# A transformer block's MLP: the second norm of token blocks 2 and 3 turned by VectorE and DMAs

## The chip, the cores and the metric

The kernel runs on one core of one Trainium2 chip. The core has TensorE (PE; its weight loads are a row of their own, PEld), VectorE (DVE), ScalarE (ACT), GpSimd (POOL) and SyncE (SP, which here issues the DMAs), with an on-chip memory of 128 partitions (SBUF), accumulation banks (PSUM) and device memory. The metric is the device time of one execution in microseconds (us), the median of several runs; lower is better.

## The reference

One block on x of 2048 tokens by 576 features, conditioned by six rows (`sa`, `ca`, `ga`, `sb`, `cb`, `gb`) worked out from a small vector `c`:

```
h = layernorm(x) * (1 + ca) + sa
x = x + ga * attention(h, wq, wk, wv, wo)          # 32 heads of 18, one shared k and v
h = layernorm(x) * (1 + cb) + sb                   # the "second norm"
y = layernorm(h)
x = x + gb * (gelu(y @ w1 + b1) @ w2 + b2)         # 576 -> 4608 -> 576
```

Everything is fp32. The second norm is in fact two norms, one behind the other (`h`, then `y`), with two rows between them.

## The kernel before, in words

**Layout.** The 2048 tokens are four blocks of 512 (`TB`), each of four tiles of 128 tokens. The residual `XT` holds tokens on the partitions. The first product of the MLP needs `y` the other way round, with features on the partitions: `yr` (128 x 10 x 512 for a pair of blocks, `KD` = 5 slices of 128 features per block, the fifth half used and filled with a second copy of its 64 features). So each tile of 128 tokens x 576 features must be normed twice and turned.

**The MLP in visits.** The MLP works on pairs of blocks: blocks 0 and 1, then blocks 2 and 3. For each pair it makes 18 visits (`NG`), each of 256 of the 4608 hidden features, 36 in all; I number them v0 to v35. A 2 x 2 scheme with seven products in place of eight is used for both matrices, and each fp32 product is made of a high and a low part. In a visit PE makes seven products of the first matrix (A11, S2, S3, A12, S1, A22, S4; `product`, L1156, into the PSUM banks `psB`) and, between them, the seven groups of the visit before for the second matrix (`fc2s`, L1247 to L1265): a group is twice 12 matmuls into one of two `psA` slots, and each slot is emptied by one DVE add (L1265). ACT and DVE make the gelu, POOL the sums and low parts (L1225 to L1233). The ACT copy at L1392 stands once near the start of each visit, so it marks its length.

**Weights.** `load_w1` (L788 to L792) and `load_w2s` (L1218 to L1223) are issued by SP, each right behind the product that used the buffer, for the next visit: there is one buffer of each, and a load has about a visit to land. SP runs its DMAs in written order.

**The end of a pair.** Visits v16, v17 and v35 make the second matrix whole (`fc2`, L1293). In v17 `op_pieces` (L1051, copies at L1069, subtractions at L1071) makes the operand pieces of blocks 2 and 3 out of `yr`: `+B11` is the first copy, `-B11` the DVE subtraction behind it.

**The second norm of blocks 2 and 3.** It is made during v1 to v16, in the gaps of the engines. `more` (L1366) is called seven times in each visit (behind A11, S2, S3, A12, S1, A22 and S4), and steps the generator `ln2_pair` (L701) once. The stages of a tile (`ln2_stages`, L658) are: `stats` (DVE: two BN_STATS and a BN_AGGR), `scale` (three small POOL operations), `norm` (ACT), `rows` (two POOL operations of 128 x 576), `stats` and `scale` again, `renorm` (two ACT operations, and b2 added to the residual on POOL), and `turn`: PE transposes (`transpose_tile`, L155 of its helper) into a `psB` bank, four of 128 columns in one step and the fifth in the next, each step emptied by ACT into `yr`. Eight tiles make 40 transposes. Tile i begins 10 steps behind tile i-1; steps with a turn are held to the third and fourth calls of a visit (`room`, `mark`). At the end two POOL operations of 128 x 1024 (L714, L716) make two sums of `yr` slices that the seven-product scheme needs.

Of the kernel before, what the change touches and what calls it, by code (L numbers as in the profile page):

```python
# [8 lines left out]
F32 = mybir.dt.float32  # L9
F32R = mybir.dt.float32r  # L10
AF = mybir.ActivationFunctionType
ALU = mybir.AluOpType
AX = mybir.AxisListType

S, D, H, DH, F = 2048, 576, 32, 18, 4608
NB = 4
TB = S // NB
NT = TB // 128
KD = 5
# [4 lines left out]
NG = F // 256  # L24
# [8 lines left out]
def block_kernel(ctx: ExitStack, tc, x, wqkv, wo, w1, b1, w2, b2, c, wmod, ident_in, out):  # L33
    nc = tc.nc
    ve, ac, po, pe, sy = nc.vector, nc.scalar, nc.gpsimd, nc.tensor, nc.sync
# [39 lines left out]
    BC = per.tile([128, 3, D], F32, name="BC")  # L75
# [5 lines left out]
    at = tc.tile_pool(name="at", bufs=1, side="right")  # L81
# [74 lines left out]

    def transpose_tile(Z, yr, t, k0, k1, e):
        p = psB()
        for k in range(k0, k1):
            tr(p[:, 128 * (k - k0):128 * (k - k0 + 1)], Z, k)  # L160
        n = k1 - k0
        src = p[:, :128 * n].rearrange("p (k c) -> p k c", k=n)
        dst = yr[:, k0:k1, 128 * t:128 * (t + 1)]
        if e is ac:
            ac.activation(dst, src, AF.Copy)
        else:
            ve.tensor_copy(dst, src)
# [329 lines left out]
    px = pxp.__enter__()  # L497
# [160 lines left out]
    def ln2_stages(tb, t):  # L658

        X = XT[:, NT * tb + t, :]  # L660
        o = {}

        def small(n):
            return per.tile([128, n], F32, name="sm2", bufs=8)

        def stats(i):
            src = o["h"] if i else X
            o["mv", i] = small(2)
            stt = ln_stats1(src)
            ve.bn_stats(stt[:, 1, :], src[:, 288:])  # L670
            ve.bn_aggr(o["mv", i], stt)

        def scale(i):
            mv, rs, nb = o["mv", i], small(1), small(1)
            po.tensor_scalar(rs, mv[:, 1:2], EPS, None, op0=ALU.add)
            po.tensor_tensor(rs, rs, nhalf, op=ALU.pow)
            po.tensor_scalar(nb, mv[:, 0:1], rs, -1.0, op0=ALU.mult, op1=ALU.mult)
            o["sc", i] = dict(scale=rs, bias=nb)

        def norm():  # L680
            Z = o["Z"] = px.tile([128, 640], F32, name="Z2", bufs=2)
            o["h"] = Z[:, :D]
            ac.activation(o["h"], X, AF.Identity, **o["sc", 0])

        def rows():
            po.tensor_mul(o["h"], o["h"], BC[:, 1, :])
            po.tensor_tensor(o["h"], o["h"], BC[:, 0, :], op=ALU.add)

        def renorm():
            ac.activation(o["Z"][:, D:], o["Z"][:, 512:D], AF.Identity, **o["sc", 1])  # L690
            ac.activation(o["h"], o["h"], AF.Identity, **o["sc", 1])
            po.tensor_tensor(X, X, B2["b"], op=ALU.add)

        def turn(k0, k1, e):
            yr = YR[tb // 2][:, KD * (tb % 2):KD * (tb % 2 + 1)]
            transpose_tile(o["Z"], yr, t, k0, k1, e)

        return {0: lambda: stats(0), 1: lambda: scale(0), 4: norm, 5: rows, 8: lambda: stats(1), 9: lambda: scale(1),
                12: renorm, 14: lambda: turn(0, 4, ac), 15: lambda: turn(4, 5, ac)}

    def ln2_pair():  # L701
        YR[1] = per.tile([128, 2 * KD, TB], F32, name="yr", tag="big", bufs=3)
        at = {}
        for _ in range(2):
            yield
        for i in range(2 * NT):
            for k, f in ln2_stages(2 + i // NT, i % NT).items():
                at.setdefault(10 * i + k, []).append((k >= 14, f))
        for k in range(max(at) + 1):
            for _, f in at.get(k, ()):  # L710
                f()
            yield "T" if any(t for t, _ in at.get(k + 1, ())) else None
        R = YR[1]
        po.tensor_tensor(R[:, 5:7], R[:, 7:9], R[:, 5:7], op=ALU.subtract)  # L714
        yield
        po.tensor_tensor(R[:, 5:7], R[:, 5:7], R[:, 0:2], op=ALU.add)  # L716
        yield

    def wo_mm(tb, t, h2, p, k0, k1, end=KD, first=0):
        A = ATT[tb]  # L720
# [190 lines left out]
    def step(q):  # L911
        if q:
            try:
                return next(q[0])
            except StopIteration:
                q.popleft()
# [218 lines left out]
    def load_w2(v):  # L1135
        w = W2[WHOLE[v]]
        if len(w) < 4:
            w.extend(px.tile([128, 640], F32R, name="Z2", bufs=2)[:, :D] for _ in range(2))
        for l in range(2):
            for f in range(2):  # L1140
                sy.dma_start(w[2 * l + f].bitcast(F32), w2scr[v % NG, :, l, f])
# [193 lines left out]
                        load_w2s(0, k)  # L1335
            yield

    fill = deque([ln2_pair()])
    f2 = deque()
    gens, sm = deque(), deque()  # L1340
    between2 = [None]
# [12 lines left out]
                gens.remove(gen)  # L1354

    form = op_pieces(YR[0], po)
    mark = [None]

    for v in range(NV):
        nxt = (v + 1) % NG  # L1360
        if v == NG - 1:
            while fill:
                step(fill)
            form = op_pieces(YR[1], po)

        def more(half="", first="", room=False):  # L1366

            if v in (0, NG - 1, NG):
                form(first if v == 0 else half if v == NG - 1 else {"+T4": "-T4 +T1 -B22", "-T4": "-T1 -t1"}.get(first, ""))
            elif v > NG + 1 and fill:  # L1370
                step(fill)
            elif 0 < v < NG and fill and (room or mark[0] != "T" or v == NG - 2):
                mark[0] = next(fill[0], "end")
                if mark[0] == "end":
                    fill.popleft()
            if v == 0 and rest:
                for _ in range(2):
                    if rest:
                        wo_tile(*rest.popleft())
                if not rest:  # L1380
                    wo_end()

        def w_(w):
            if v + 1 < NV:
                load_w1(nxt, w)

        if v == NG + 1:
            fill.append(pair_end())
        ba = psB()
        product(ba, "A11", 0)  # L1390
        w_("A11")
        ac.activation(U[:, 0], ba, AF.Copy)  # L1392
        g_()
        s_()
        more("+B11", "+T4")
        bb = psB()
        product(bb, "S2", 6, mid=t_ if v > 1 and v - 1 not in WHOLE and v - 2 not in WHOLE else None)
        w_("S2")
        ve.tensor_tensor(U[:, 0], bb, U[:, 0], op=ALU.add)
        if v != 1:  # L1400
            t_()
        g_()
        more("-B11 +T2", "-T4")
        bc = psB()
        product(bc, "S3", 10)
        w_("S3")
        ve.tensor_tensor(U[:, 1], bc, U[:, 0], op=ALU.add)
        s_()
        more("-T2 =T3", "+B22", True)
        if v != 1:  # L1410
            t_()
        product(ba, "A12", 2, False, (0, 0))
        w_("A12")
        gens.append(gelu(v, 0, 0, ba))
        g_()
        s_()
        more("+T3 +B21", "-B22", True)
        t_()
        g_()
        bd = psB()  # L1420
        product(bd, "S1", 8, True, (1, 1))
        w_("S1")
        be = psB()
        ve.tensor_tensor(be, bd, U[:, 1], op=ALU.add)
        g_()
        gens.append(gelu(v, 1, 1, be))
        g_()
        more("-T3 -B21")
        t_()
        g_()  # L1430
        product(bc, "A22", 12, False, (1, 0), t_ if v == 1 else None)
        w_("A22")
        ve.tensor_tensor(bc, bc, U[:, 0], op=ALU.add)
        g_()
        gens.append(gelu(v, 1, 0, bc))
        g_()
        more("=T4 +t0")
        t_()
        if v - 1 in WHOLE:
            t_()  # L1440
        g_()
        product(bd, "S4", 4, False, (2, 1), t_ if v == 1 else None)
        w_("S4 tails")
        if v == NV - 1:
            t_(lambda: (eb_add(NV - 2, 1, 1, (0,)), g_()))
        ve.tensor_tensor(bd, bd, U[:, 0], op=ALU.add)
        if v < NV - 1:
            g_()
        gens.append(gelu(v, 0, 1, bd))
        g_()  # L1450
        if v < NV - 1:
            t_()
        more("=T1 +T4 -t0 +B22 +t1")
        if v == NV - 1:
            last = fc2(v)
            next(last)
            t_(lambda: next(last))
            for to in ((1, 0, (1,)), (1, 1, (1,))):
                eb_add(NV - 2, *to)
            while gens:  # L1460
                g_()
            eb_add(NV - 2, 0, 1)
            f2.append(last)
            continue
        if v - 1 in WHOLE:
            while f2:
                t_()
        if v not in WHOLE:
            sm.append(sums(v))
            s_()  # L1470
            f2.append(fc2s(v))
        else:
            f2.append(fc2(v))
# [42 lines left out]
```

## Time and profile before

| | |
|---|---|
| median of 3 runs | 2223.07 us (2222.27 to 2224.61) |
| profiled execution, its own time | 2222.87 us |
| its span | 2221.0 us |
| busy: PE, PEld, DVE, ACT, POOL | 99%, 65%, 87%, 74%, 69% |
| MLP visits of the first pair | v0 to v17, some 23 us each |
| 40 PE transposes, L155 | inside v3 to v16 |

The span is what the hardware profiler saw from the first instruction to the last; 1.9 us lie around it. Busy shares are means over stages that differ, so a visit has to be read by itself.

### The profile page before, as it was taken

How to read it: one execution, taken by the hardware profiler on the slowest of the kernel's cores; microseconds unless marked ns; L12 is line 12 of the kernel's file. 1: busy time of each engine (PE TensorE's matmuls, PEld its weight loads, DVE VectorE, ACT ScalarE, POOL GpSimd, SP SyncE). 2: the span in 40 equal slices, each digit the busy share in tenths (PEclk: the TensorE clock that was granted, in tenths of full speed). 3: DMA queues.
4: the chain of work that ended last, by engine and by line, in shares of the span. 5: the costliest groups of instructions: out<-in, count | busy, mean ns of one | idle time of the engine just before them, and what ended most of it. 6: DMA issues, size and time to landing. Idle time of an engine off the chain costs nothing.

```text
span 2221.0 us, 46122 instructions
## 1 busy us (share of the span) xinstructions
PE 2201.4 (99%) x16643; PEld 1449.3 (65%) x16643; DVE 1932.7 (87%) x3415; ACT 1639.2 (74%) x3144; POOL 1526.4 (69%) x1762
## 2 busy tenths in 40 slices
PE   8999999999999999999999999999999999999999
PEld 5654444444544545444454446888888899889898
DVE  7689999999999999999999983888888878788887
ACT  5569999999999999999999998544445444343443
POOL 7654455666776687678676540888888867877776
PEclk9999999999999999999999999999999999999999
DMA  6242143443333332333333321666666646676663
GB/s 228 86 133 92 34 134 117 135 129 116 126 119 118 115 130 97 112 130 111 117 127 117 120 70 63 207 178 175 179 179 180 184 128 182 180 219 189 178 183 123
DMA packets 184632, 307.71 MB, mean 139 GB/s; under 512 B 19695, under 2 KB 75391, under 8 KB 184405
## 3 DMA queue, kind: packets, MB, share of 16 engines
q1 hardware_dynamic: 184261, 304.62, 43.9%
q8 instruction: 132, 2.16, 0.4%
q14 instruction: 95, 0.78, 0.1%
q10 hardware_dynamic: 144, 0.15, 0.0%
HBM read 200.68 MB, written 93.79 MB: 133 GB/s over the span
## 4 chain that ended last, share of the span: by engine, by line
PE 93%; DVE 1%; ACT 1%; issue 0%; ACTq 0%; DVEq 0%
PE psC L932 24%; PE psB L1156 18%; PE psA L1259 16%; PE psB L942 14%; PE psM L319 13%; PE psB L731 2%; PE psB L952 2%; PE psA L1293 1%; PE psA L731 1%; PE psB L155 0%; PE psB L248 0%; PE psB L357 0%; PE psM L942 0%; ACT P L944 0%; DVE mx L344 0%; DVE gs L1168 0%
## 5 line engine op out<-in xcount | busy, mean ns | idle before, releaser
L944 ACT ACTIVATE P<-psB 128x512 f32<-128x512 f32 x2013 | 1054.4, 619 | 42.3 <-PE psM L319 20.6
L964 DVE TENSOR_REDUCE mx<-psM 128x1 f32<-128x512 f32 x1476 | 934.3, 682 | 28.5 <-PE psM L319 15.6
L942 PE MATMUL psB<-qst,KS 64*128 64x512 f32 x2013 | 605.1, 433 | 0.1
L319 PE MATMUL psM<-KS,qst 64*128 64x512 f32 x1722 | 590.2, 434 | 0.7 <-DVE mx L337 0.2
L932 PE MATMUL psC<-P,V 128*32 128x256 f32 (+3 forms) x6608 | 568.1, 439 | 0.0
L942 PEld LDWEIGHTS psB<-qst,KS 64*128 64x128 f32 x2013 | 301.7, 184 | 218.6 <-ACT P L944 186.2
L319 PEld LDWEIGHTS psM<-KS,qst 64*128 64x128 f32 x1722 | 283.5, 184 | 185.6 <-DVE mx L964 130.3
L1156 PE MATMUL psB<-ops,w1a 128*128 128x512 f32 x1512 | 393.9, 396 | 0.2 <-DVE h L1171 0.2
L1156 PEld LDWEIGHTS psB<-ops,w1a 128*128 128x128 f32 x1512 | 270.1, 188 | 46.7 <-DVE h L1171 0.6
L932 PEld LDWEIGHTS psC<-P,V 128*32 128x32 f32 x6608 | 147.0, 108 | 187.7 <-issue 160.2
L1265 DVE TENSOR_TENSOR XT<-psA,XT 128x576 f32<-128x576 f32 x330 | 241.8, 753 | 18.6 <-PE psA L1259 13.2
L1259 PEld LDWEIGHTS psA<-w2s,big 128*128 128x128 f32 x1584 | 223.0, 188 | 14.0 <-POOL big L1233 2.5
L1259 PE MATMUL psA<-w2s,big 128*128 128x288 f32 x1584 | 230.5, 294 | 0.0
L1169 ACT ACTIVATE psB<-gs 128x512 f32<-128x512 f32 x144 | 86.7, 602 | 127.6 <-DVE gs L1168 127.4
L1233 POOL TENSOR_TENSOR big<-s,big 128x512 fp32r<-128x512 f32 x132 | 171.0, 1295 | 10.6
L962 DVE CUSTOM_DVE_ANT_0 xc<-psM,xc 128x512 f32<-128x512 f32 x246 | 166.3, 682 | 12.9 <-PE psM L319 4.4
L1165 ACT ACTIVATE h<-psB,b1t 128x512 f32<-128x512 f32 x144 | 98.1, 681 | 100.7 <-PE psB L1156 76.7
L768 POOL TENSOR_TENSOR os<-O,os 128x512 fp32r<-128x512 f32 x31 | 39.8, 1285 | 171.8 <-ACT os L767 171.8
L955 ACT ACTIVATE xc<-psB 128x512 f32<-128x512 f32 x246 | 154.1, 626 | 3.0 <-PE psM L319 0.2
L1168 DVE SCALAR_TENSOR_TENSOR gs<-psB,h 128x512 f32<-128x512 f32 x144 | 98.6, 684 | 38.5 <-ACT psB L1166 38.4
L802 POOL TENSOR_TENSOR r<-r,r 128x256 fp32r<-128x256 f32 (+1 forms) x162 | 121.8, 752 | 13.0
L1174 ACT ACTIVATE big<-h 128x512 fp32r<-128x512 f32 x39 | 24.7, 634 | 133.8 <-DVE h L1171 133.8
(217 smaller groups left out, 3327.5 us busy)
## 6 DMA issues: line engine op xcount, KB each, us to landing
w1a<-w1scr SPq DMA_DIRECT2D x252, 256.0 KB
w2s<-w2sum SPq DMA_DIRECT2D x132, 288.0 KB
w1scr<-r SPq DMA_DIRECT2D x126, 256.0 KB
w2s<-w2scr SPq DMA_DIRECT2D x76, 288.0 KB
w2scr<-r SPq DMA_DIRECT2D x72, 288.0 KB
w2sum<-r SPq DMA_DIRECT2D x72, 288.0 KB
qst<-qscr SPq DMA_DIRECT2D x192, 72.0 KB
w1a<-w2scr SPq DMA_DIRECT2D x33, 288.0 KB
```

What stands on the lines that cost most here:

```text
L319: pe.matmul(o, QST[n][64 * g:64 * g + 64, p, 128 * qt:128 * (qt + 1)], KS[64 * g:64 * g + 64, 512 * kb:512 * (kb + 1)], start=True, stop=True)
L802: po.tensor_tensor(o[:, n:2 * n], src, o[:, :n].bitcast(F32), op=ALU.subtract)
L932: pe.matmul(PVt[n][32 * j:32 * (j + 1), cs], V[:, kc, :], t[:, j, cs], start=(kc == 0 and h0 == 0), stop=(kc == 15), skip_group_check=True)
L942: pe.matmul(t, KS[64 * g:64 * g + 64, 128 * kc:128 * (kc + 1)], QST[n][64 * g:64 * g + 64, i, :], start=True, stop=True)
L944: ac.activation(P[n, kc][:, 2 * i + g, :], t, AF.Exp, scale=SCALE)
L955: ac.activation(XC[-1], t, AF.Relu)
L962: ve.tensor_tensor_reduce(c, t, c, 1.0, -3.0e38, ALU.add, ALU.max, o)
L964: ve.tensor_reduce(o, t, axis=AX.X, op=ALU.max)
L1156: pe.matmul(o, x, y, start=(first and i == 0), stop=(i == len(terms) - 1), skip_group_check=True)
L1233: po.tensor_tensor(unit(u, 1), x, unit(u, 0).bitcast(F32), op=ALU.subtract)
L1259: pe.matmul(p[:, i, :288], x[:, ts_], W2S[k][:, y], start=(bool(first) and q == 0), stop=(q == 2), skip_group_check=True)
L1265: ve.tensor_tensor(o, p[:, :, :288], o, op=ALU.add)
```

## The change

The eight tiles of blocks 2 and 3 are no longer turned by PE.

- `turn` is one DVE operation for a tile, `ve.transpose` of 128 x 576 (L693 of the new file), which turns each 32 x 32 square in its place. Its result goes to `T`, a third row of the tile `BC`. There is one `T`.
- `spread` (L695) brings the squares to their partitions of `yr`: 24 DMAs from SBUF to SBUF per tile, all issued by SP, six at each of four calls. Per tile there are 8 of 32 x 5 x 32 elements (L702), 8 of 32 x 4 x 32 (L704) and 8 of 32 x 32 (L707). A contiguous piece is 32 fp32 values, 128 bytes, so a tile has 8 x 160 + 8 x 128 + 8 x 32 = 2,560 pieces; the eight tiles make 192 DMAs.
- The copy of the last 64 features (one ACT operation of 128 x 64 per tile) and the ACT emptying of the PE transposes go; the tile buffer `Z2` is 576 wide in place of 640.
- `less` makes the two sums on POOL per 128 tokens (128 x 2 x 128 elements) instead of 128 x 1024 at the end, each for tokens t of both blocks.
- The generator with its marks is replaced by `ln2_plan`: a table `when` gives each tile the visits of its five steps. `turn` stands at the third call of visits 4, 5, 8, 9, 12, 13, 15 and 16, and the spreads at calls four to seven of the same visit; `stats`, `scale`, `rows`, `norm` and `renorm` get calls of their own. The last `less` stands at the start of v17, ahead of the first copy of `op_pieces`.

The core of the diff:

```diff
@@ ln2_stages
         def norm():
-            Z = o["Z"] = px.tile([128, 640], F32, name="Z2", bufs=2)
-            o["h"] = Z[:, :D]
+            o["h"] = px.tile([128, D], F32, name="Z2", bufs=2)
             ac.activation(o["h"], X, AF.Identity, **o["sc", 0])
...
         def renorm():
-            ac.activation(o["Z"][:, D:], o["Z"][:, 512:D], AF.Identity, **o["sc", 1])
             ac.activation(o["h"], o["h"], AF.Identity, **o["sc", 1])
             po.tensor_tensor(X, X, B2["b"], op=ALU.add)
 
-        def turn(k0, k1, e):
-            yr = YR[tb // 2][:, KD * (tb % 2):KD * (tb % 2 + 1)]
-            transpose_tile(o["Z"], yr, t, k0, k1, e)
...
+        def turn():
+            ve.transpose(T, o["h"])
+
+        def spread(i):
+            yr = YR[1][:, KD * (tb % 2):KD * (tb % 2 + 1), 128 * t:128 * (t + 1)]
+            for n in range(i, 24, 4):
+                p, q = divmod(n, 6)
+                rs, cs = slice(32 * p, 32 * p + 32), slice(32 * p, 32 * p + 32)
+                if q < 2:
+                    sy.dma_start(yr[32 * q:32 * q + 32, :, cs], wide[rs, :, 64 + 32 * q:96 + 32 * q])
+                elif q < 4:
+                    sy.dma_start(yr[32 * q:32 * q + 32, :KD - 1, cs],
+                                 T[rs, :512].rearrange("f (k c) -> f k c", c=128)[:, :, 32 * q:32 * q + 32])
+                else:
+                    sy.dma_start(yr[32 * q - 64:32 * q - 32, KD - 1, cs], T[rs, 32 * q + 384:32 * q + 416])
+
+        def less():
+            R = YR[1][:, :, 128 * t:128 * (t + 1)]
+            po.tensor_tensor(R[:, 5:7], R[:, 7:9], R[:, 5:7], op=ALU.subtract)
+            po.tensor_tensor(R[:, 5:7], R[:, 5:7], R[:, 0:2], op=ALU.add)
+
+        T = BC[:, 2, :]
...
+    def ln2_plan():
...
+        when = ((1, 1, 2, 3, 4), (2, 2, 3, 4, 5), (5, 5, 6, 7, 8), (6, 6, 7, 8, 9), (9, 9, 10, 11, 12, 13, 6),
+                (10, 10, 11, 12, 13, 15, 4), (11, 12, 13, 14, 15, 16, 5), (13, 13, 14, 15, 16, NG - 1, 0))
+        turns = [w[4] for w in when]
+        for i, (v0, v1, v2, v3, v4, *end) in enumerate(when):
+            stats, scale, norm, rows, renorm, turn, spread, less = ln2_stages(2 + i // NT, i % NT)
+            at(v0, 4, stats, 0)
+            at(v1, 5, scale, 0)
+            at(v1, 6, norm)
+            at(v2, 4, rows)
+            at(v3, 4 if v3 in turns else 3, stats, 1)
+            at(v3, 5, scale, 1)
+            at(v3, 6, renorm)
+            at(v4, 3, turn)
+            for j in range(4):
+                at(v4, 4 + j, spread, j)
+            if end:
+                at(*end, less)
+        return plan
...
     for v in range(NV):
         nxt = (v + 1) % NG
+        calls = iter(range(1, 8))
+        if v == 1:
+            plan = ln2_plan()
         if v == NG - 1:
-            while fill:
-                step(fill)
+            planned(v, 0)
             form = op_pieces(YR[1], po)
...
-            elif 0 < v < NG and fill and (room or mark[0] != "T" or v == NG - 2):
-                mark[0] = next(fill[0], "end")
-                if mark[0] == "end":
-                    fill.popleft()
+            elif 0 < v < NG:
+                planned(v, next(calls))
```

The lines of the MLP stand 26 lower in the new file (L1265 becomes L1291, L792 becomes L818, L1223 becomes L1249).

What stands on SP in the middle of a visit of the first pair, before: the loads of the next visit's weights alternate, L792 those of the first matrix (the second `w1a` row here is that of A12) and L1223 those of the second.

```order
L1223 DMA w2s<-w2sum 128x576
L792 DMA w1a<-w1scr 128x512
L1223 DMA w2s<-w2scr 128x2x288
L792 DMA w1a<-w1scr 128x512
L1223 DMA w2s<-w2scr 128x2x288
L792 DMA w1a<-w1scr 128x512
```

The same place in a visit with a turn, now: `BC` is the row `T`, `yr` the operand of blocks 2 and 3.

```order
L1249 DMA w2s<-w2sum 128x576
L818 DMA w1a<-w1scr 128x512
L702 DMA yr<-BC 32x5x32
L707 DMA yr<-BC 32x32
L704 DMA yr<-BC 32x4x32
L702 DMA yr<-BC 32x5x32
L707 DMA yr<-BC 32x32
L704 DMA yr<-BC 32x4x32
L1249 DMA w2s<-w2scr 128x2x288
L818 DMA w1a<-w1scr 128x512
```

Six DMAs have come between the A12 load and the loads behind it; three more batches of six follow in the visit, each behind the next `w1a` load.

What stands on DVE at the start of visits in which a tile gets its second `stats`, before: `psA` adds (L1265) around the three stats operations, and the second gelu operation (L1168) and the S2 addition (L1399) of the visit.

```order
L1171 SCALAR_TENSOR_TENSOR h<-psB,h 128x512
L1265 TENSOR_TENSOR XT<-psA,XT 128x2x288 x2
L143 BN_STATS bst<-Z 128x6
L670 BN_STATS bst<-Z 128x6
L671 BN_AGGR sm<-bst 128x2
L1168 SCALAR_TENSOR_TENSOR gs<-psB,h 128x512
L1265 TENSOR_TENSOR XT<-psA,XT 128x2x288 x2
L1399 TENSOR_TENSOR u<-psB,u 128x512
```

On DVE in v5, the second of two visits with a turn, now (L1437 is the addition behind S3, L1407 before; L1197 and L1194 are the gelu's).

```order
L1197 SCALAR_TENSOR_TENSOR h<-psB,h 128x512
L1437 TENSOR_TENSOR u<-psB,u 128x512
L693 STREAM_TRANSPOSE BC<-Z 128x576
L1291 TENSOR_TENSOR XT<-psA,XT 128x2x288 x2
L143 BN_STATS bst<-XT 128x6
L670 BN_STATS bst<-XT 128x6
L671 BN_AGGR sm<-bst 128x2
L1291 TENSOR_TENSOR eb<-psA,eb 128x576 x2
L1194 SCALAR_TENSOR_TENSOR gs<-psB,h 128x512
```

The stats have left the start of the visit for its middle, and the turn stands ahead of two adds that empty `psA` slots.

## Rows read from the trace of the kernel before

**Rows 1.** The page, busy time of each engine: us, share of the span, instructions.

```profile
PE 2201.4 (99%) x16643; PEld 1449.3 (65%) x16643; DVE 1932.7 (87%) x3415; ACT 1639.2 (74%) x3144; POOL 1526.4 (69%) x1762
```

**Rows 2.** Two visits by window: length, busy PE PEld DVE ACT POOL, clock, DMA share, GB/s.

```profile
1450.00:1500.00 50.00, 50.00 (x297) 44.69 (x297) 39.63 (x62) 23.49 (x40) 44.19 (x45) 1.00 0.62 177
```

**Rows 3.** ACT timeline, L1392, v3, v16, v21, v22: start, duration, engine, line, [idle before].

```profile
1442.92 0.60 ACT L1392 ACTIVATE u<-psB 128x512 f32<-128x512 f32 x1
...
1744.16 0.60 ACT L1392 ACTIVATE u<-psB 128x512 f32<-128x512 f32 x1
...
1862.13 0.60 ACT L1392 ACTIVATE u<-psB 128x512 f32<-128x512 f32 x1 [0.18 <-PE psB L1156]
...
1884.91 0.60 ACT L1392 ACTIVATE u<-psB 128x512 f32<-128x512 f32 x1 [0.17 <-PE psB L1156]
```

**Rows 4.** PEld timeline, the two turns of one tile in a visit.

```profile
1494.80 0.59 PEld L155 LDWEIGHTS psB<-ident,Z 128*128 128x128 f32 x4
...
1498.71 0.14 PEld L155 LDWEIGHTS psB<-ident,Z 128*128 128x128 f32 x1
```

**Rows 5.** Waits of PEld, 1400 to 2200 us: us in total, times, longest.

```profile
PEld psA L1259 <- POOL big L1233: 2.5, 7, 0.4
```

**Rows 6.** SP timeline of the visit that begins at 1466.27.

```profile
1466.27 0.32 SPq L792 DMA_DIRECT2D w1a<-w1scr  x1
...
1475.43 0.32 SPq L792 DMA_DIRECT2D w1a<-w1scr  x1
1477.52 0.52 SPq L1223 DMA_DIRECT2D w2s<-w2scr  x1
...
1487.86 0.32 SPq L1223 DMA_DIRECT2D w2s<-w2sum  x1
```

**Rows 7.** Lines of SP: count, ns min/median/max, starts; last row timeline of one four.

```profile
L772 SPq DMA_DIRECT2D big<-os x112: 765/789/897, 203.4 to 1351.9; - x112
L779 SPq DMA_DIRECT2D big<-os x12: 697/711/775, 469.0 to 1084.9; - x12
L364 SPq DMA_DIRECT2D qst<-ms x128: 620/638/911, 125.7 to 1332.2; - x128
L315 SPq DMA_DIRECT2D qst<-qscr x192: 265/313/1562, 39.2 to 1264.7; - x192
...
316.02 3.33 SPq L772 DMA_DIRECT2D big<-os  x4
```

**Rows 8.** Waits of SP for a DMA to land: us in total, times, longest.

```profile
SPq L540 <- DMA rowscr<-bc: 3.0, 3, 1.0
```

**Rows 9.** DVE's transposes of the attention and its stats, by line.

```profile
L749 DVE STREAM_TRANSPOSE T<-O x32: 700/702/711, 174.6 to 1372.9; 128x512 f32<-128x512 f32 x32
...
L143 DVE BATCH_NORM_STATS2 bst<-Z x16: 449/450/460, 555.6 to 1744.7; 128x6 f32<-128x288 f32 x16
```

**Rows 10.** DVE and PEld timelines of v21, which begins at 1862.13.

```profile
1868.09 0.69 DVE L1407 TENSOR_TENSOR u<-psB,u 128x512 f32<-128x512 f32 x1
...
1871.11 1.78 PEld L1259 LDWEIGHTS psA<-w2s,gt 128*128 128x128 f32 x12
...
1872.36 1.56 DVE L1265 TENSOR_TENSOR BC<-psA,BC 128x576 f32<-128x576 f32 x2 [1.93 <-PE psA L1259]
```

**Rows 11.** ACT, DVE and PEld timelines of v17.

```profile
1768.24 0.61 ACT L1392 ACTIVATE u<-psB 128x512 f32<-128x512 f32 x1
...
1769.46 1.05 ACT L1069 ACTIVATE ops<-yr 128x1024 fp32r<-128x1024 f32 x1
...
1771.96 2.38 DVE L1071 TENSOR_TENSOR ops<-yr,ops 128x1024 fp32r<-128x1024 f32 x1
...
1777.64 1.41 DVE L1330 TENSOR_TENSOR XT<-psA,XT 128x576 f32<-128x576 f32 x2
...
1778.57 0.55 PEld L1293 LDWEIGHTS psA<-w2s,gt 128*128 128x128 f32 x3
```

**Rows 12.** The page, the queue of SP's DMAs: packets, MB, share of 16 engines.

```profile
q1 hardware_dynamic: 184261, 304.62, 43.9%
```

More of the change, by code (lines that the diff above doesn't have):

```diff
@@ L689, in renorm @@
         def renorm():
-            ac.activation(o["Z"][:, D:], o["Z"][:, 512:D], AF.Identity, **o["sc", 1])
             ac.activation(o["h"], o["h"], AF.Identity, **o["sc", 1])
             po.tensor_tensor(X, X, B2["b"], op=ALU.add)
-        def turn(k0, k1, e):
-            yr = YR[tb // 2][:, KD * (tb % 2):KD * (tb % 2 + 1)]
-            transpose_tile(o["Z"], yr, t, k0, k1, e)
-        return {0: lambda: stats(0), 1: lambda: scale(0), 4: norm, 5: rows, 8: lambda: stats(1), 9: lambda: scale(1),
-                12: renorm, 14: lambda: turn(0, 4, ac), 15: lambda: turn(4, 5, ac)}
@@ L701, in ln2_pair @@
-    def ln2_pair():
-        YR[1] = per.tile([128, 2 * KD, TB], F32, name="yr", tag="big", bufs=3)
[L703 to L717, printed above, removed]
+        def turn():
+            ve.transpose(T, o["h"])
@@ new lines, in less, with at @@
+        def less():
[3 more added lines that the diff above has]
+        T = BC[:, 2, :]
+        wide = BC.rearrange("p r d -> p (r d)")[:, 2 * D - 64:].rearrange("f (k c) -> f k c", c=128)
+        return stats, scale, norm, rows, renorm, turn, spread, less
+    def ln2_plan():
+        YR[1] = per.tile([128, 2 * KD, TB], F32, name="yr", tag="big", bufs=3)
+        plan = {}
+        def at(v, c, f, *a):
+            plan.setdefault((v, c), []).append(lambda: f(*a))
+        when = ((1, 1, 2, 3, 4), (2, 2, 3, 4, 5), (5, 5, 6, 7, 8), (6, 6, 7, 8, 9), (9, 9, 10, 11, 12, 13, 6),
[16 more added lines that the diff above has]
+        return plan
@@ L1137, in load_w2 @@
         if len(w) < 4:
-            w.extend(px.tile([128, 640], F32R, name="Z2", bufs=2)[:, :D] for _ in range(2))
+            w.extend(px.tile([128, D], F32R, name="Z2", bufs=2) for _ in range(2))
         for l in range(2):
@@ L1336, in fc2 @@
             yield
-    fill = deque([ln2_pair()])
+    fill = deque()
+    plan = {}
     f2 = deque()
@@ L1356, in block_kernel, with planned, more @@
     form = op_pieces(YR[0], po)
-    mark = [None]
+    def planned(*when):
+        for f in plan.pop(when, ()):
+            f()
     for v in range(NV):
         nxt = (v + 1) % NG
+        calls = iter(range(1, 8))
+        if v == 1:
+            plan = ln2_plan()
         if v == NG - 1:
-            while fill:
-                step(fill)
+            planned(v, 0)
             form = op_pieces(YR[1], po)
-        def more(half="", first="", room=False):
+        def more(half="", first=""):
             if v in (0, NG - 1, NG):
@@ L1408, in block_kernel @@
         s_()
-        more("-T2 =T3", "+B22", True)
+        more("-T2 =T3", "+B22")
         if v != 1:
@@ L1416, in block_kernel @@
         s_()
-        more("+T3 +B21", "-B22", True)
+        more("+T3 +B21", "-B22")
         t_()
```

## The prediction

> **What bounds the kernel now.** The page first: PE is busy 99% of the span and every other engine less [rows 1], so a gain must come out of PE's own work or its few waits, and a loss is whatever makes PE wait. Second the stage: the change touches v1 to v17 alone, and in two of these visits PE has no gap, DVE and POOL are near 80 and 88%, ACT under half, the DMA engines at 62%, at a full granted clock [rows 2]. Third the length of a visit, which the ACT copy marks: in the second pair, where no norm is made beside it, a visit takes 1884.91 - 1862.13 = 22.78 us; in the first pair v3 to v15 take 1744.16 - 1442.92 = 301.24, against 13 x 22.78 = 296.1 [rows 3]. So the second norm now costs 5.1 us over the seven tiles turned there, 0.73 each. That is the prize: 8 x 0.73 = 5.8 us.
>
> **What is removed.** A tile's five transposes hold PE's loads for 0.59 + 0.14 = 0.73 us [rows 4], part of it beside other loads; the rest of the 5.1 is waits in front of `psA` groups, 2.5 us gross in seven places [rows 5], at visit starts, where the three stats operations stand ahead of adds that empty a slot. Both go: the turn leaves PE, and the stats move to calls three and four. I take the whole 5.8 as gain. At the least the waits stay, for 8/7 x 2.5 = 2.9 less; at the most a few tenths more go, since the work of ACT that falls away hid behind PE anyway.
>
> **What is added on DVE.** A DVE transpose of 128 x 512 takes 0.70 [rows 9], so 576 columns take 0.79. It follows the addition behind S3, which ends 1868.78 - 1862.13 = 6.65 into a visit, and stands ahead of two `psA` adds of 0.78 each (half of 1.56); behind them DVE sat idle 1.93 us [rows 10]. In the first turn of a couple the transpose is ready to start, and with the stats, two operations of 0.45 [rows 9] and a shorter one, 1.1, it needs 1.9 of the 1.93. The first of the two adds ends at rel 6.65 + 0.79 + 0.78 = 8.2 then, and PE wants its slot at 1871.11, rel 8.98 [rows 10]: it fits, cost nothing. If that cover were gone, eight turns would cost at most 8 x 0.8 = 6. POOL's work is the same in sum; in v3, v7, v11 and v14, where `rows` and other steps meet, its idle time is about used up, and a wait of the size of rows 5's longest, 0.4, in each would be 1.6 us; I take nothing.
>
> **What is added on SP, the term that decides.** 24 DMAs a tile from SBUF to SBUF. Before, SP issues such DMAs in three lines: L772 (18 partitions x 2 pieces of 2 KB) holds SP for 0.789 us, L779 (18 pieces) 0.711, L364 (8 pieces of 512 bytes) 0.638; the same 18-partition form out of device memory takes 0.313; between two issues lie (3.33 - 4 x 0.789) / 3 = 0.058 [rows 7]. None has 32 partitions or 128-byte pieces, so the price is open from both sides: 0.31 from the device-memory line, and 1.3 if it grows with pieces as it does from L779 to L772 (0.078 for 18 pieces, 4.3 ns each; 160 pieces 1.32, 128 pieces 1.19, 32 pieces 0.77). I take the rows of the same kind of transfer: 0.789 for the sixteen with many pieces a partition, 0.711 for the eight with one: 18.3, and 24 x 0.058 = 1.4, so 19.7 us a tile.
>
> Where they stand: the first batch is behind the A12 load, issued by rel 1475.75 - 1466.27 = 9.5 of the visit [rows 6]. Among the four batches SP also issues the weights that stood there, seven rows from 0.52 to 0.32 between the A12 load and 1488.18, 3.1 in all [rows 6], with gaps 3.6 at the most. SP is then never idle, and the last piece is issued at 9.5 + 19.7 + 3.6 = 32.8; a landing takes about 1.1 behind that (SP's own waits for one, 1.0 [rows 8]): 33.9. But there is one `T`, and the turn of the next visit may not write it until all 24 have read it. It wants to at 22.78 + 6.65 = 29.4. DVE waits at the turn to 33.9, is done at 34.7, and empties the first slot at 35.5; PE wanted that slot at 22.78 + 8.98 = 31.8. Queued behind the waiting transpose are both adds, the stats and the gelu's second operation, and PE stands until the slot is empty: 3.7 us. Such couples are v4 and v5, v8 and v9, v12 and v13, v15 and v16: 4 x 3.7 = 14.8. The weight loads behind the batches come up to some 10 us late; each has nearly a visit (22.78) until its product, less its landing, so I cost that at nothing; a delay past 18 would turn into PE waits of its own.
>
> **The tail in v17.** The A12 load of v16 is issued at 22.78 + 9.5 + 3.7 = 36.0 on the same scale, and the last pieces land 19.7 + 3.6 + 1.1 later, at 60.4; v17 begins at 2 x 22.78 + 3.7 = 49.3, so they land at rel 11.1. `+B11` reads that part of `yr` at 1769.46 - 1768.24 = 1.2, 9.9 earlier. Two slacks soften it: DVE began `-B11` 1.45 behind that copy's end, and the first add of L1330 (half of 1.41) ended 0.2 before PE used the slot [rows 11]. Everything behind it on DVE stands in line: 9.9 - 1.65 = 8.3 us of PE.
>
> **The sum**, against the profiled execution's own 2222.87 (0.2 below the median of the runs): -5.8 + 14.8 + 8.3 = +17.3, so 2240.2, call it 2240. With 0.76 to 0.9 us per DMA, the spread of L772's own times, each 0.04 is 1 us a tile, 4 in the couples and 1 in the tail, and the slack terms add 3: 2231 to 2254.
>
> **Rivals.**
> *Quick issue (the other side: faster).* SP pays 0.31 to 0.39 for such a DMA, as it does for device memory. Then a tile is 24 x 0.39 = 9.4 us, SP idles between batches, and the last is issued just behind the last weights of the visit; `T` is free at 26 to 27, before 29.4, and in v17 the pieces come at most 1 us late: 2222.9 - 5.8 + 0.5 = 2217.5. For it: 32 partitions are another shape than 18 or 8, and the price may hang on that. Against it: all 252 transfers of rows 7's first three lines take 0.62 or more, and the 18-partition shape out of device memory is cheap, so it is not the 18. [...]
> *In between.* At 0.62 per DMA a tile is 24 x 0.678 = 16.3, the couples lose 0.3 each and the tail about 5: the loss eats the gain, 2220 to 2227. This is the point from which the sign turns.
> *Issue grows with pieces.* At 4.3 ns a piece a tile takes 8 x (1.32 + 1.19 + 0.77) + 1.4 = 27.7, 8 longer: 11.7 a couple, 46.8, and 16 in the tail: -5.8 + 46.8 + 16 = 57, 2280; with half that growth 2260.
> *The DMA engines are the bound.* 2,560 pieces a tile at the queue's mean packet, 0.439 x 16 x 2221 us / 184,261 = 85 ns [rows 12], are 13.6 us of 16 engines, which at 62% busy already have 0.38 free; by bytes (0.33 MB at 177 / 0.62 = 285 GB/s) they are 1.2. From nothing, then, to 13.6 / 0.38 = 36 us a tile and 2300; half way is about the 19 us of the forecast by another route. [...]
>
> **How the numbers follow.** The forecast 0.37; quick issue 0.36, of which 0.33 faster; in between 0.09; growth with pieces 0.14; the DMA engines 0.04. A measurement of this kernel can tell 0.2% (4.4 us) from no change. Faster 0.33, the same 0.03 + 0.09 = 0.12, slower 0.37 + 0.14 + 0.04 = 0.55. The time is the forecast's, 2240, with its own 2231 to 2254; the range takes in quick issue below (2216) and most of the growth above (2272), which leaves out the dearer end of growth and of the DMA engines.
>
> **What would show it.** In SP's rows the time of one issue at L702, L704 and L707: about 0.75 by the forecast, 0.35 by quick issue, over 1.1 by growth. In DVE's rows the transposes of v5, v9, v13 and v16 start late behind a DMA, and PE waits some 3.7 us at a `psA` group that follows; v4, v8, v12 and v15 show none. In v17 the first copy waits for a DMA for 8 to 10 us. Visits without a turn, v6 or v10, take 22.8. The forecast is wrong if SP idles between batches, if the second transposes start where the first do, or if PE waits in visits that have no turn.

## The result, and the profile after

The changed kernel takes 2233.97 us (median of 6 runs, 2230.62 to 2236.05) against 2222.96 (6 runs, 2221.38 to 2224.61): a ratio of 1.0047, with a 95% interval of 1.0036 to 1.0058. It is slower by 11.0 us; 17 were forecast. The profiled execution took 2230.95, 8.1 more than the profiled one of before.

The engines' busy time has hardly moved, PE by 40 instructions less [rows 1]:

```profile
PE 2199.6 (99%) x16603; PEld 1446.6 (65%) x16603; DVE 1937.2 (87%) x3423; ACT 1628.7 (73%) x3120; POOL 1525.8 (68%) x1768
```

So the visits have to be read. The ACT copy that marks a visit's start (L1422 now), at the starts of v3, v4, v5, v6, v16, v17 and v18:

```profile
1441.81 0.60 ACT L1422 ACTIVATE u<-psB 128x512 f32<-128x512 f32 x1
...
1464.69 0.60 ACT L1422 ACTIVATE u<-psB 128x512 f32<-128x512 f32 x1 [0.20 <-PE psB L1182]
...
1487.46 0.60 ACT L1422 ACTIVATE u<-psB 128x512 f32<-128x512 f32 x1 [0.20 <-PE psB L1182]
...
1511.34 0.60 ACT L1422 ACTIVATE u<-psB 128x512 f32<-128x512 f32 x1 [0.19 <-PE psB L1182]
...
1742.21 0.60 ACT L1422 ACTIVATE u<-psB 128x512 f32<-128x512 f32 x1 [0.20 <-PE psB L1182]
...
1768.55 0.60 ACT L1422 ACTIVATE u<-psB 128x512 f32<-128x512 f32 x1
...
1801.81 0.60 ACT L1422 ACTIVATE u<-psB 128x512 f32<-128x512 f32 x1 [0.68 <-PE psB L1182]
```

v4, with a first turn, takes 22.77, the clean length; v5, with a second turn, 23.88. From v3 to v16 it is 300.40 where it was 301.24 [rows 3]: the whole gain of 5.1 is there, and 4.3 of it is spent again, 1.1, 1.7 and 1.2 in v5, v9 and v13 and 0.2 in v12. v16 and v17 together take 59.60; before, v17 began at 1744.16 + 24.08 and v18 at 1793.71, 49.55 for the two. That is 10.05 more, and the loss. (The start of v0 differs by up to 1.1 us either way among all kernels below, whose programs are the same up to there; here it came 1.1 earlier. -1.1 - 0.8 + 10.05 = 8.1.)

SP's price, the term that decided. The three forms of DMA, with 160, 128 and 32 pieces, in SP's rows (count, ns min/median/max, starts):

```profile
L702 SPq DMA_DIRECT2D yr<-BC x64: 592/599/1352, 1474.0 to 1773.9; - x64
L704 SPq DMA_DIRECT2D yr<-BC x64: 595/606/621, 1475.4 to 1773.3; - x64
L707 SPq DMA_DIRECT2D yr<-BC x64: 559/599/1301, 1474.8 to 1775.2; - x64
```

0.60 to 0.61 us each by the medians, whatever the pieces: neither the 0.79 and 0.71 of the nearest rows nor the 0.31 from device memory [rows 7]. What it does to the couple v4 and v5, in the timelines of SP, DVE and PEld (start, duration, engine, line, [idle before]):

```profile
1474.05 0.69 SPq L702 DMA_DIRECT2D yr<-BC  x1
...
1483.29 0.58 SPq L1249 DMA_DIRECT2D w2s<-w2scr  x1
...
1493.73 1.30 SPq L707 DMA_DIRECT2D yr<-BC  x1
...
1493.42 0.69 DVE L1437 TENSOR_TENSOR u<-psB,u 128x512 f32<-128x512 f32 x1
1496.21 0.78 DVE L693 STREAM_TRANSPOSE BC<-Z 128x576 f32<-128x576 f32 x1 [2.10 <-DMA yr<-BC]
1496.91 1.39 DVE L1291 TENSOR_TENSOR XT<-psA,XT 128x576 f32<-128x576 f32 x2
...
1497.68 0.43 PEld L1285 LDWEIGHTS psA<-w2s,gt 128*128 128x128 f32 x3 [1.28 <-DVE XT L1291]
```

Here the reader sees the chain of the forecast: SP issues without a gap from 1474.05 to 1495.03, 21 us for 24 DMAs and the weights between them; the turn of v5 waits 2.10 for the readers of `T`; the `psA` add behind it is late; PE stands for 1.28. (The last of the 24 held SP for 1.30 here; why is not shown.) The lines of v16, the same two places of the last couple:

```profile
1752.49 0.78 DVE L693 STREAM_TRANSPOSE BC<-Z 128x576 f32<-128x576 f32 x1 [3.63 <-DMA w1a<-w1scr]
...
1753.96 1.62 PEld L1285 LDWEIGHTS psA<-w2s,gt 128*128 128x128 f32 x12 [2.82 <-DVE XT L1291]
```

SP was done with the tile before at 1749.73, 30.3 us behind the start of v15, as in the couple v4 and v5 (30.3). But the turn begins 2.8 us after that, where in v5 it was 1.2. The row names a load of `w1a`; by the trace's landing events, sixteen for each DMA, fifteen shares of the last piece had landed by 1750.86, and the last at 1752.17. So the stall of a couple is SP's time and the landing of the last piece together.

The tail, in the timelines of SP, POOL, ACT and PEld in v17, and the window behind it (columns as in [rows 2]):

```profile
1775.15 0.56 SPq L707 DMA_DIRECT2D yr<-BC  x1
...
1778.57 0.72 POOL L711 TENSOR_TENSOR yr<-yr 128x256 f32<-128x256 f32 x1 [9.69 <-DMA w1a<-w1scr]
1779.37 0.72 POOL L712 TENSOR_TENSOR yr<-yr 128x256 f32<-128x256 f32 x1
...
1769.92 1.05 ACT L1095 ACTIVATE ops<-yr 128x1024 fp32r<-128x1024 f32 x1
1780.12 1.06 ACT L1095 ACTIVATE ops<-yr 128x1024 fp32r<-128x1024 f32 x1 [7.46 <-POOL yr L712]
...
1784.29 0.74 PEld L1319 LDWEIGHTS psA<-w2s,gt 128*128 128x128 f32 x3 [5.82 <-DVE XT L1356]
```

```profile
1784.00:1789.00 5.00, 4.71 (x16) 4.38 (x17) 4.92 (x8) 3.89 (x6) 1.40 (x1) 0.50 0.00 0
```

The last piece is issued at 1775.71 and POOL's sum of the last tile, which needs it, begins 2.9 later. (The row names the weights of `w1a` as releaser. By the landing events it was the piece itself: fourteen of its sixteen shares had landed by 1777.17, the last at 1778.42; of the `w1a` load issued behind it the first share landed only at 1778.55. The DMA engines were 42% busy in these 2.9 us.) ACT's copy behind the sum, DVE's subtraction and the adds stand in line, and PE waits 5.82. After that PE runs 5 us at a granted clock of 0.50, where it was 1.00 from 1775.71 to 1778.57: by an estimate from that row, half of the 4.71 busy, some 2.4 us more.

### The profile page after: what moved, and what is told of

It is laid out like the page before. It is cut to its first block, busy times and chain, and to the rows that moved or that the text cites. A ratio compares the mean times of both kernels' runs of the same rounds, so it can differ in the third digit from the quotient of the medians.

```text
span 2228.8 us, 46291 instructions
## 1 busy us (share of the span) xinstructions
PE 2199.6 (99%) x16603; PEld 1446.6 (65%) x16603; DVE 1937.2 (87%) x3423; ACT 1628.7 (73%) x3120; POOL 1525.8 (68%) x1768
## 4 chain that ended last, share of the span: by engine, by line
PE 91%; DVE 1%; ACT 1%; DMA 1%; SPq 1%; issue 0%; POOL 0%; DVEq 0%; ACTq 0%; POOLq 0%
PE psC L958 24%; PE psB L1182 18%; PE psA L1285 16%; PE psB L968 14%; PE psM L319 13%; PE psB L757 2%; PE psB L978 2%; PE psA L1319 1%; PE psA L757 1%; PE psB L248 0%; PE psB L357 0%; DMA yr<-BC 0%; DMA Z<-w2scr 0%; PE psM L968 0%; ACT P L970 0%
## 5 line engine op out<-in xcount | busy, mean ns | idle before, releaser
L1291 DVE TENSOR_TENSOR XT<-psA,XT 128x576 f32<-128x576 f32 x330 | 241.3, 751 | 16.1 <-PE psA L1285 10.5
L1259 POOL TENSOR_TENSOR big<-s,big 128x512 fp32r<-128x512 f32 x132 | 170.8, 1294 | 10.6
L1194 DVE SCALAR_TENSOR_TENSOR gs<-psB,h 128x512 f32<-128x512 f32 x144 | 98.8, 686 | 38.9 <-ACT psB L1192 38.8
```

Of the source, the lines that this page charges most:

```text
L1259: po.tensor_tensor(unit(u, 1), x, unit(u, 0).bitcast(F32), op=ALU.subtract)
L1291: ve.tensor_tensor(o, p[:, :, :288], o, op=ALU.add)
```

## The experiments

The kernel before took 2222.85 (27 runs) beside the first four and 2222.91 (27 runs) beside the last four.

**Sixteen DMAs.** The turned tile is 640 wide with the last 64 features doubled, so the eight small DMAs fall into the others; the diff shows the DMAs alone.

```diff
-            for n in range(i, 24, 4):
-                p, q = divmod(n, 6)
...
+            for n in range(i, 16, 4):
+                p, q = divmod(n, 4)
+                rs, cs = slice(32 * p, 32 * p + 32), slice(32 * p, 32 * p + 32)
+                sy.dma_start(yr[32 * q:32 * q + 32, :, cs], wide[rs, :, 32 * q:32 * q + 32])
```

> The tile that is turned is 640 wide again (ACT copies the last 64 features before the turn), so a tile is spread by 16 DMAs of 32 x 5 x 32 instead of 24 of three sizes: the same 2,560 pieces of 128 bytes, a third fewer issues. Theory (SP's time per issue, 0.60 + 0.05 us each, times the count): a tile takes 8 x 0.65 = 5.2 us less of SP, T is free at 31.5 - 5.2 = 26.3 us after the first turn's visit began, before the second turn wants it at 29.4, so v5, v9, v13 and v16 lose their stalls (1.1 + 1.7 + 1.2 + about 3) and v17 its 5.8 us with the half clock behind it: 2216 to 2219, 0.2% under the kernel before. Rival A (landing and the DMA engines, set by the number of pieces): the same pieces, so 2230 to 2236 as the changed kernel. Rival B (the turn and the stats at their new places on DVE, or POOL's smaller sums): nothing changes, or a little worse by the 64 columns more, 2234 to 2236.

Measured 2223.38 (11 runs), ratio 1.0001 (0.9992 to 1.0010). Against the changed kernel that is 10.6 less, the way of the theory, but not down to its 2216 to 2219. v5, v9 and v13 take 22.94, 22.92 and 22.99: the couples' stalls are gone. v17 still takes 28.79 against 25.47. The timelines of SP and POOL there say why:

```profile
1757.50 2.02 SPq L1164 DMA_DIRECT2D w2s<-w2scr  x4
...
1763.75 0.90 SPq L1164 DMA_DIRECT2D w2s<-w2scr  x2
1764.74 0.86 SPq L1164 DMA_DIRECT2D Z<-w2scr  x2
1765.64 2.53 SPq L704 DMA_DIRECT2D yr<-BC  x4
...
1772.01 0.74 POOL L708 TENSOR_TENSOR yr<-yr 128x256 f32<-128x256 f32 x1 [6.15 <-DMA w1a<-w1scr]
```

The last four are issued by 1768.17, behind eight loads of whole second matrices (288 KB each), and POOL's sum begins 3.8 us later: in this one place it is the landing, as rival A has it, that is late: the DMA engines were 99% busy from 1768.17 to 1772.01, and 88% over the 10 us from 1765 to 1775.

**One DMA per tile.** `if i == 0: sy.dma_start(yr, wide)` in place of the sixteen. It leaves out bringing the squares to their partitions, so what it computes is not the MLP; it shows the time alone.

> As the sixteen-DMA kernel, but one DMA of 128 x 5 x 128 per tile instead of sixteen (640 pieces of 512 bytes): the squares are not brought to their partitions, which is left out of the computation; DVE's turns, the stats and POOL's sums stand where they stand. Theory: SP has 1 issue per tile, no stall is left, 2216 to 2219, within 1.5 us of the kernel with sixteen. Rival A: clearly below the kernel with sixteen, since the small pieces are gone. Rival B: the loss stays, 2230 or more.

Measured 2219.18 (10 runs), ratio 0.9982 (0.9973 to 0.9991). v17 takes 25.11. So the turn on DVE, the moved stats and the smaller sums are not the loss, and rival B falls: all of it is in bringing the pieces over. Visits with a turn take 22.93 to 22.95 here and v12 23.66, where the changed kernel has 22.77 to 22.78 in v4, v8 and v15 and 23.01 in v12; the kernels with the 640-wide tile turn 64 columns more and have ACT's copy back.

**Thirty-two DMAs.** Each of the sixteen cut in two: `for ks in (slice(0, 3), slice(3, KD))`.

> As the sixteen-DMA kernel, each DMA cut in two (3 and 2 of the five slices): 32 issues per tile, the same pieces and bytes. Theory: 8 x 0.65 = 5.2 us more of SP per tile than the changed kernel, so v5, v9, v13 and v16 stall 5.2 longer each (6.3 to 8 us) and the last pieces come 5.2 later in v17: 2234 + 20.8 + 5.2 = 2260 (2252 to 2268). Rival A: the same pieces, 2230 to 2236. Rival B: 2230 to 2236.

Measured 2265.7 (4 runs), ratio 1.0190 (1.0177 to 1.0204). Same pieces, same bytes, 42 us more than with sixteen: the count of issues decides, and rival A falls for the couples. In v5 SP issued the last piece by 1500.91, and the turn began at 1502.12 after a wait of 7.46. The waits of PEld, 1380 to 1830 us (us in total, times, longest):

```profile
PEld psA L1283 <- DVE XT L1289: 22.0, 6, 6.1
PEld psB L1180 <- DMA w1a<-w1scr: 8.9, 8, 1.7
PEld psA L1317 <- DVE XT L1354: 8.3, 1, 8.3
```

The second line is new: with eight issues more, the weights behind them come too late for their products.

**Sixteen for the last two tiles alone.** `if tb == 3 and t > 1:` the sixteen, else the 24; all tiles are 640 wide.

> The changed kernel, but the last two tiles (turned in v15 and v16) are spread by 16 DMAs; the first six by 24 as before. Theory: the stalls of v5, v9 and v13 stay (1.1 + 1.7 + 1.2 = 4.0 us), those of v16 and v17 go with the half clock behind them (10 us of the two visits): 2223 to 2225, level with the kernel before. Rival A: 2230 to 2236. Rival C (v17 is late for another reason than the last pieces, such as POOL's sums or the waiting weights): v17 stays near 33 us, 2229 to 2233.

Measured 2228.3 (10 runs), ratio 1.0021 (1.0012 to 1.0030), above what I expected: v5 and v9 keep their stalls (24.90 and 24.36), v13 most of its own (23.61), v16 is clean at 23.87, but v17 takes 29.52: as with sixteen throughout, POOL's sum begins late, at 1776.04, when the last issue had ended at 1773.09. v5 lost 2.1 here and 1.1 in the changed kernel with the same 24 DMAs: its last piece landed 2.8 us after the issue instead of 1.2, fifteen of the sixteen shares by 1496.70 and the last at 1498.37.

**The last tile's DMAs earlier.** On top of the sixteen:

```diff
-                at(v4, 4 + j, spread, j)
+                at(v4, 4 + (j // 2 if i == 2 * NT - 1 else j), spread, j)
```

> The sixteen-DMA kernel, but the last tile's DMAs (v16) are issued eight and eight at calls four and five instead of four at each of calls four to seven, so ahead of the whole second matrices (2 MB) that SP loads in the rest of v16. What is left of the loss there is 3.3 us in v17 (28.79 against 25.47): the last four DMAs were issued by 1768.17 and POOL's sum, which needs them, began at 1772.01, 3.8 us later, with the DMA engines 88% busy. Theory (the last pieces queue behind weights on the DMA engines): they land before v17, v17 takes 25.1 to 25.5 as with one DMA per tile, 2219 to 2221. Rival (v17 waits for the weights or POOL, whichever way the pieces come): v17 stays at 28 to 29, 2223.

Measured 2219.63 (11 runs), ratio 0.9983 (0.9974 to 0.9992): faster than before. v17, from its own start to v18's:

```profile
1766.17 0.60 ACT L1419 ACTIVATE u<-psB 128x512 f32<-128x512 f32 x1
...
1791.28 0.60 ACT L1419 ACTIVATE u<-psB 128x512 f32<-128x512 f32 x1 [0.68 <-PE psB L1179]
```

25.11, as with one DMA. The same sixteen, ahead of the big loads instead of behind them, land in time. They are also issued sooner, the last by 1763.02 in place of 1768.17; that the queue on the DMA engines was the brake rests on the 3.8 us and the 99% above, not on this run alone.

**A norm moved.** On top of that, the seventh tile's first norm goes from call six of v12 to call two of v13.

```diff
-            at(v1, 6, norm)
+            at(v1 + (i == 6), 2 if i == 6 else 6, norm)
```

> As the kernel with the last tile early, and the first norm of the seventh tile on ACT moved from call six of v12, where another tile's renorm stands, to call two of v13. In v12 every kernel with the new plan takes 23.65 instead of 22.78, also that with one DMA per tile: ACT's two norms of 0.87 stand ahead of a gelu, DVE idles 1.2 and PE 0.87. Theory: v12 takes 22.8 and nothing is late elsewhere, 0.8 us less than the kernel with the last tile early: 2218.5 to 2220. Rival (ACT is as tight in v13): the 0.8 comes back there, no difference.

Measured 2218.71 (11 runs), ratio 0.9980 (0.9972 to 0.9989). The place that it cures, ACT in v12 of the kernel with one DMA per tile, where two norms (L692 and L684) and a copy stand ahead of a gelu operation (L1190):

```profile
1668.92 0.43 ACT L691 ACTIVATE Z<-Z,sm,sm 128x64 f32<-128x64 f32 x1
1669.38 0.87 ACT L692 ACTIVATE Z<-Z,sm,sm 128x576 f32<-128x576 f32 x1
1670.16 0.85 ACT L684 ACTIVATE Z<-XT,sm,sm 128x576 f32<-128x576 f32 x1
1670.92 0.58 ACT L1190 ACTIVATE psB<-gs 128x512 f32<-128x512 f32 x1
```

v12 went from 23.69 to 22.96, v17 from 25.11 to 25.58. The 0.9 us between the medians lie inside both intervals, so it is not shown that this last step helps as a whole.

**A later second turn, 24 DMAs.** The changed kernel, with the second turn of the first three couples one call later.

```diff
+            late = i in (1, 3, 5)
-            at(v4, 3, turn)
+            at(v4, 4 if late else 3, turn)
             for j in range(4):
-                at(v4, 4 + j, spread, j)
+                at(v4, min(5 + j, 7) if late else 4 + j, spread, j)
```

> The changed kernel with its 24 DMAs per tile, but the second turn of the first three couples (v5, v9, v13) stands at call four instead of three, and its DMAs at calls five, six and seven (six, six and twelve). T is free 31.5 us after the first turn's visit began; at call three the turn was wanted at 29.4, at call four not before 33. Theory (the wait is for T alone): the stalls of v5, v9 and v13 go, 1.1 + 1.7 + 1.2 = 4.0, while v16 and v17 stay: 2230. Rival (SP's load as such is the cost, by way of the weights that stand behind 24 DMAs, or DVE has no room there): the 4 us stay or move to the next visit, 2234.

Measured 2228.48 (11 runs), ratio 1.0023 (1.0014 to 1.0032), 5.5 under the changed kernel. The three visits are 3.8 us shorter in the traces. v5 is clean; its start and v6's:

```profile
1488.67 0.60 ACT L1423 ACTIVATE u<-psB 128x512 f32<-128x512 f32 x1 [0.20 <-PE psB L1183]
...
1511.44 0.60 ACT L1423 ACTIVATE u<-psB 128x512 f32<-128x512 f32 x1 [0.17 <-PE psB L1183]
```

22.77, with the same 24 issues and the same weights behind them; v9 and v13 take 22.78 and 23.01. The turn still waits there for `T` (0.94, 0.77 and 0.24), but the two `psA` adds now stand ahead of it. So in these three couples the cost was the adds behind the turn's wait for `T`, not SP's load as such. v16 and v17 kept theirs (27.48 and 33.71).

**The price of an issue by shape.** Eighteen DMAs of 64 columns more, in v7 of the sixteen-DMA kernel; each line stands in a loop of three.

```diff
+            sy.dma_start(T[0:18, cs], BC[0:18, 0, cs])
+            sy.dma_start(T[32:64, cs], BC[32:64, 0, cs])
+            sy.dma_start(T[96:128, cs], BC[0:32, 0, cs])
+            sy.dma_start(T[64:96, cs], w1scr[0, 0:32, 0, 0:64])
+            sy.dma_start(T[:, cs], BC[:, 0, cs])
+            sy.dma_start(T[0:8, cs], BC[0:8, 0, cs])
```

> The sixteen-DMA kernel with 18 DMAs more at call four of v7, back to back, each of 64 columns into the free T (nothing uses them): SBUF to SBUF with 18, 32 (to the same and to other partitions), 128 and 8 partitions, and device memory to SBUF with 32 partitions, three of each. Theory (SBUF to SBUF is what makes an issue 0.6, whatever the shape): all but the device-memory three take 0.55 to 0.8, those 0.3. [...]

By line, in that order (18 partitions, 32, 32 to others, 32 from device memory, 128, 8):

```profile
L744 SPq DMA_DIRECT2D BC<-BC x3: 698/798/881, 1543.1 to 1544.9; - x3
L747 SPq DMA_DIRECT2D BC<-BC x3: 570/583/590, 1545.6 to 1546.8; - x3
L750 SPq DMA_DIRECT2D BC<-BC x3: 588/588/589, 1547.5 to 1548.7; - x3
L753 SPq DMA_DIRECT2D BC<-w1scr x3: 405/419/582, 1549.4 to 1550.5; - x3
L756 SPq DMA_DIRECT2D BC<-BC x3: 536/599/600, 1550.9 to 1552.1; - x3
L759 SPq DMA_DIRECT2D BC<-BC x3: 625/687/712, 1552.8 to 1554.3; - x3
```

The source and the number of partitions both have a share: from SBUF an issue cost 0.17 more than from device memory at 32 partitions, and 18 partitions 0.2 more than 32 or 128. These are three issues of each form in a single run (2220.33 us).

## Why the prediction came out right, step by step

The chain of the forecast is the one that the traces show, and its 2231 to 2254 hold the measured 2233.97. But 11.0 us (8.1 in the profiled execution) are not 17.3: the price per issue was a quarter too high, 0.76 on the mean against 0.60, and part of that was made up by weights, landings and a half clock that the sum did not have. That the time fell inside its range is in part luck.

- **The prize** was right for the seven tiles from v3 to v15: without the 4.0 lost in v5, v9 and v13 they take 296.4 in place of 301.24, 4.8 of the 5.1. That the eighth gives its 0.7 is not shown. With one DMA per tile the seven take 298.14 and the kernel 3.7 less, since its wider tiles cost what is said there.
- **DVE at no cost** was right: v4, v8 and v15 of the changed kernel, each with a turn, take the clean 22.77 to 22.78.
- **SP's price** was mis-sized twice. 24 DMAs were costed at 19.7 by rows of 18 partitions and took 16.2 in v4 and v5, most at 0.60 + 0.05 and the last at 1.30; the weights between them were costed at 3.6 and took 4.8, since in a queue without gaps five of the eight held SP for 0.53 to 0.58, where before none took more than 0.52. From first issue to last 21.0 against 23.3.
- **The couples**: where and how was right (second turns late behind a DMA, PE late at a `psA` group, nothing in v4 or in v6). The size was not: `T` was free at rel 31.5, 32.2, 31.8 and 33.0, not 33.9, so the first three lost 1.1 to 1.7 each instead of 3.7 and v16 2.3 over its time before, 6.3 in all against 14.8. The step from `T` to PE held: `T`'s time + 0.79 + 0.78 - 31.8 gives 1.3, 2.0, 1.6 and 2.8, and PE stood 1.28, 1.93, 1.13 and 2.82. The landing, put at 1.1, took from 1.2 to 2.8.
- **The tail** had the right sum by luck, 8.3 for v17 against 33.26 - 25.47 = 7.8, by a chain that was wrong in two places. `+B11` began on time (1769.92, rel 1.37), since it reads block 2 and the last tile is of block 3; late was the next copy, behind POOL's `less`. And PE stood 5.8, not 8.3; the half clock after it made up the rest, which the forecast had not in it.
- **The rivals.** Growth with pieces falls by the equal rows of L702, L704 and L707, and quick issue, at 0.31 to 0.39, by the same rows. The DMA engines as a bound fall for the couples by the thirty-two, but not for the last pieces in v17 of the kernel with sixteen. The measured 0.60 lies beside the 0.62 that "in between" named as the turning point. That point expected 2220 to 2227: it put the tail at 5, and the dearer weights, the landings over 1.1 and the half clock at nothing. So the price fell into the middle case and the time into the forecast's own range.

What stays open: the changed kernel's runs spread over 5.4 us, those of the kernel with one DMA per tile over 2.6; which of the stalls varies was not traced run by run, but v5 at 1.1 and 2.1 in two kernels shows that a couple's landing does. What holds back the last shares is not shown either; in v16 and in v17 one 16 KB packet of the instruction queue was on the DMA engines while they were late (from 1750.14 to 1751.07 and from 1775.33 to 1776.41), and no run takes it away.

## What to carry to other kernels

Many small DMAs were paid by their count on the engine that issues them (the same pieces by 16, 24 and 32 a tile: 2223.38, 2233.97 and 2265.7): widen a tile or double a few columns if that makes 16 out of 24, before looking at bytes. The single buffer between two steps that stand a visit apart made the whole queue ahead of it part of the critical path (the turn of v5 waited 2.10, PE behind it 1.28), and moving its writer by one call was enough in three couples (3.8 us in the kernel with the later turn). What the next stage needs first was better issued ahead of bulk loads that have slack: behind them, in v17 of the kernel with sixteen, POOL's sum began 3.8 us after the last issue and the kernel took 2223.38, ahead of them 2219.63.

## What the runs showed of the hardware

SP's time for an SBUF-to-SBUF DMA did not depend on its pieces (32, 128 and 160 pieces, 0.60, 0.61 and 0.60 by the medians of L707, L704 and L702). By source and partitions SP's time for a DMA differed: 0.42 from device memory with 32 partitions, and from SBUF 0.58 to 0.60 for 32 and 128 partitions, 0.69 for 8, 0.80 for 18 (three issues each, back to back, in one run). 18 partitions out of device memory, at 0.313 [rows 7], show no such surcharge. What makes 8 and 18 partitions dearer from SBUF is not shown.

After PE had stood for 5.8 us the granted clock was 0.50 for the next 5 us; after a wait of 2.3, in the kernel with sixteen DMAs, it was 0.74 in one window of 5 us (1780 to 1785). The price of these two stalls is then not their length alone.
